# Half-height transposes in the attention, and a weight part fetched in 512-byte pieces, in a fused attention and expert kernel

## The chip, the cores and the metric

The kernel runs on one core of a Trainium2 chip. The time is device microseconds of one execution; three plain runs of the kernel before took 727.77 to 731.6 us, the median is 728.2 us. One further execution was recorded by the hardware profiler. Its engines are named PE (TensorE; PEld is its weight load, which runs beside it), DVE (VectorE), ACT (ScalarE), POOL (GpSimd) and SP (SyncE, which only issues transfers here).

## The reference, cut to what matters

```python
def _attn_ref(q, k, v):                       # 4 batches, 8 heads, 576 positions, 64 dims
    scores = scale * np.matmul(q, k.transpose(0, 1, 3, 2))
    rel = pos[:, None] - pos[None, :]
    mask_local = (rel >= 0) & (rel < 32)                              # heads 0 to 3
    mask_strided = (rel >= 0) & (pos[None, :] % 32 == pos[:, None] % 32)   # heads 4 to 7
    ...
    return np.matmul(softmax(np.where(masks, scores, -1e9)), v)

def _moe_ref(x, ...):                         # 2304 tokens, 8 experts, 512 -> 1024 -> 512
    logits = x @ w_gate + modality_bias[modality_id]
    e_idx = np.argmax(logits, axis=1)
    for e in range(E):
        h = np.maximum(x[e_idx == e] @ w1[e], 0.0)
        out[e_idx == e] = gate_w * (h @ w2[e])

def _moe2_ref(x, w_in, w_out):                # dense: 512 -> 2048 -> 512, ELU between
    h = x @ w_in
    return np.where(h > 0, h, np.exp(np.minimum(h, 0)) - 1) @ w_out
```

## The kernel before

The program has three stages. The attention takes some 110 us; the experts' stage and the dense one, which are long rows of fp32r products on TensorE, take the rest.

**Attention.** The work goes by pairs of heads: 4 batches with 4 pairs each, 16 in all, in the order `PAIRS = [2, 0, 3, 1]`, so that a strided pair (heads 4 to 7) and a local pair (heads 0 to 3) take turns. Even numbers n are strided, odd ones local. The order on every engine is the order in which the code is written, and it is pipelined by hand. Iteration n holds: `emit_S(n)`, the scores of pair n, with mask and maximum on VectorE (L1274, L1277) and the subtraction of the maximum on GpSimd (L1278); `emit_T(n + 1, 0)` and `(n + 1, 1)`, which transpose q of the next pair; `emit_PT(n - 1)`, which transposes the probabilities P of the pair before; `emit_T(n + 1, 2)` and `(n + 1, 3)` for k; `emit_PV(n - 1)`, P times v, divided by the row sums on VectorE (L1336, L1365); `emit_X(n - 2)`, which transposes the attention's result x for the router; and the exponential of pair n on ScalarE (L1283). After every fourth pair (in the local iterations 5, 9 and 13) the router's logits follow (L1413, L1424). For local pairs ScalarE first relays q and k into another layout (L1119).

A strided pair packs two heads and two halves of the rows into quarter tiles of 64 rows by 64 columns on TensorE (L1252, L1332); a full transpose takes 128 rows (L1291, L1307, L1393, L1399) or 96 (L1228, L1236). Every transpose writes to a PSUM bank, from which ScalarE or VectorE copies. The banks are handed out in turn from three tags; P's, PV's and x's share four under the tag "P":

```python
t = psum.tile([128, 512], F32, tag=tag, bufs={"S": 2, "T": 2, "P": 4}[tag], name=name)
```

**P and x before.** P of a strided pair (`sm_s`, 128 rows, 12 blocks) is transposed in six full transposes into two banks, three and then three; P of a local pair (`sm_l`, 9 blocks of 96) in nine into three banks, four, four and the tail (L1307). x of a strided pair takes six full transposes (L1393), x of a local pair four (L1399) and, for its tail, two plain 64 x 64 products with the identity (L1402) into a bank of their own; ScalarE copies both banks (L1404).

**First expert job.** After batch 1 the routing of the first two batches runs in the background of the attention (`early`). It picks the expert of the first job, gathers its tokens from DRAM on GpSimd (L467), and fetches the weights of the first blocks of 128 hidden units on SP. `fetch` issues two transfers per block, one of w1 (rows of 512 bytes, L496) and one of w2 (rows of 2 KB, L498), into one of three buffers `wraw`; ScalarE and VectorE split a buffer in a high and a low part (L489, L490), which frees it. Three fetches are issued by iteration 15, the fourth when the first split has run.

Of the kernel before, what the change touches and what calls it, by code (L numbers as in the profile page):

```python
# [19 lines left out]
B, H, S, D = 4, 8, 576, 64  # L20
# [397 lines left out]
def ffn(tc, ctx, tc_dram, x_dram, ident, router, conv, bank, w1, w2, out, run_attention):  # L418
# [75 lines left out]
    def fetch(job, f):  # L494
        raw = wr_p.tile([128, 1024], F32, tag="wraw", name="wraw")
        nc.sync.dma_start(raw[:, 0:512].rearrange("p (k n) -> p k n", k=4),  # L496
                          w1[bass.ds(job.e, 1)].rearrange("e (k p) f -> p (e k) f", p=128)[:, :, f * 128:(f + 1) * 128])
        nc.sync.dma_start(raw[:, 512:1024], w2[bass.ds(job.e, 1)].rearrange("e f d -> (e f) d")[f * 128:(f + 1) * 128])  # L498
        return raw

    def gemm1(job, f, i, ps=None):
# [570 lines left out]
def attention(tc, bg, q, k, v, mod, mbias, wg, x_dram, ident, router, bank):  # L1072
# [212 lines left out]
    def emit_PT(n):  # L1285
        if pairs[n][1] >= 2:
            sm, pt = sm_s, pt_s
            for r in range(2):
                ps = bank("P", "ps_p")
                for z in range(Z):  # L1290
                    nc.tensor.transpose(ps[:, 128 * z:128 * z + 128], sm[:, 384 * r + 128 * z:384 * r + 128 * z + 128], ident)  # L1291
                nc.scalar.copy(pt[:, Q6 * r:Q6 * (r + 1)].rearrange("p (b q) -> p b q", q=N3),
                               ps.rearrange("p (b q) -> p b q", q=D)[:, 0:6, 0:N3])
            rs = m_p.tile([128, 12], F32, tag="rs", name="rs")
            nc.vector.reduce_sum(rs, rss[n], axis=AX.X)
            bg()
            nc.vector.tensor_scalar(rs, rs, 1e-9, None, ALU.add)
            bg()
            rec = m_p.tile([128, 2, 6], F32, tag="rec", name="rec")
            nc.vector.reciprocal(rec.rearrange("p w (z r) -> p r z w", r=2), rs.rearrange("p (r z w) -> p r z w", r=2, w=2))  # L1300
            bg()
            rss[n] = rec
            return
        for at, cnt in ((0, 4), (TAIL + 1, 4), (TAIL, 1)):
            ps = bank("P", "ps_p")[0:KW, 0:128 * cnt]
            for i in range(cnt):
                nc.tensor.transpose(ps[:, 128 * i:128 * i + 128], sm_l[:, at + i], ident)  # L1307
            (nc.scalar.copy if cnt > 1 else nc.vector.tensor_copy)(pt_l[:, at:at + cnt].rearrange("p s q -> p (s q)"), ps)

    xs, stores = {}, []  # L1310

# [2 lines left out]
    def emit_PV(n):  # L1314
# [9 lines left out]
        if strided:  # L1324
            pss = [bank("P", "ps_v", 128, 6, D) for w in range(2)]
            for z in range(Z):
                for r in range(2):
                    for x in range(2):
                        for w in range(2):
                            ro = slice(64 * w, 64 * w + N3)  # L1330
                            at = (6 * r + 2 * z + x) * N3
                            nc.tensor.matmul(pss[w][64 * x:64 * x + 64, 2 * z + r], lhsT=pt_s[ro, at:at + 64],  # L1332
                                             rhs=vs[pr - 2][ro, 3 * x + z, D * r:D * r + D], start=True, stop=True)
            rec = rss.pop(n)
# [14 lines left out]
        for r in range(2):  # L1349
            for s in range(4):  # L1350
                for x in range(2):
                    nc.tensor.matmul(pss[r][64 * x:64 * x + 64, s], lhsT=pt_l[:, parts[r][0] + s, 64 * x:64 * x + 64],
                                     rhs=vl[pr][:, 2 * s + x, r], start=True, stop=True)
        for r in range(2):
            nc.tensor.matmul(pss[0][64 * r:64 * r + 64, TAIL], lhsT=pt_l[:, TAIL, 64 * r:64 * r + 64],
                             rhs=vl[pr][:, 8, r], start=True, stop=True)
        rs = m_p.tile([128, 9], F32, tag="rs", name="rs")
        for ps, (i, j) in zip(pss, parts):
# [22 lines left out]
    def emit_X(n):  # L1381

        b, pr = pairs[n]
        h0 = 2 * (pr % 2)
        x_sb = xs[b, pr // 2]
        if n + 2 >= NP:
            store_x(len(stores))
        if pr >= 2:
            for a in range(2):
                ps = bank("P", "ps_x")[:, 0:384]  # L1390
                o = ps.rearrange("p (q x z) -> p z x q", x=2, z=Z)
                for z in range(Z):
                    nc.tensor.transpose(o[:, z], x_sb[:, 2 * z + a, h0:h0 + 2].rearrange("p h d -> p (h d)"), ident)  # L1393
                nc.scalar.copy(xt[:, pr].rearrange("p j (i u a) -> p a j i u", i=R3, a=2)[:, a],
                               ps[:, 0:6 * N3].rearrange("p (i j u) -> p j i u", i=R3, u=6))
            return
        ps, pe = bank("P", "ps_x"), bank("P", "ps_xe", 128, D)
        for s in range(4):
            nc.tensor.transpose(ps[:, 128 * s:128 * s + 128], x_sb[:, 4 * s + h0:4 * s + h0 + 2].rearrange("p h d -> p (h d)"), ident)  # L1399
        for r in range(2):  # L1400
            ro = slice(64 * r, 64 * r + 64)
            nc.tensor.matmul(pe[ro], lhsT=x_sb[ro, 16 + pr], rhs=ident[ro, ro], start=True, stop=True)  # L1402
        for t, i, j in ((ps, 0, 16), (pe, 16, J)):
            nc.scalar.copy(xt[:, pr, i:j, 0:32], t.rearrange("p (j c) -> p j c", c=32))  # L1404

    lgt = const.tile([128, 2 * S], F32, name="lgt")

# [93 lines left out]
```

## Time and profile before

| what | value |
|---|---|
| median of three plain runs | 728.2 us (727.77 to 731.6) |
| profiled execution: its own time | 735.35 us |
| its span, first to last instruction | 733.6 us |
| TensorE busy | 713.0 us (97%) |
| TensorE's weight load busy | 626.4 us (85%) |
| VectorE busy | 554.4 us (76%) |
| ScalarE busy | 418.2 us (57%) |
| GpSimd busy | 120.4 us (16%) |
| TensorE's granted clock, mean | 0.984 |

The span leaves out what lies before the first and after the last instruction, 1.75 us. Ends of matmuls are modelled, so a stream of them overlaps itself: what one costs in a row is read from start to start. A clock of 1.00 is 2.4 GHz, 0.50 is 1.2 GHz; a figure between is a mean over a stretch.

### The profile page before, as it was taken

How to read it: one execution, taken by the hardware profiler on the slowest of the kernel's cores; microseconds unless marked ns; L12 is line 12 of the kernel's file. 1: busy time of each engine (PE TensorE's matmuls, PEld its weight loads, DVE VectorE, ACT ScalarE, POOL GpSimd, SP SyncE). 2: the span in 40 equal slices, each digit the busy share in tenths (PEclk: the TensorE clock that was granted, in tenths of full speed). 3: DMA queues.
4: the chain of work that ended last, by engine and by line, in shares of the span. 5: the costliest groups of instructions: out<-in, count | busy, mean ns of one | idle time of the engine just before them, and what ended most of it. 6: DMA issues, size and time to landing. Idle time of an engine off the chain costs nothing.

```text
span 733.6 us, 13503 instructions
## 1 busy us (share of the span) xinstructions
PE 713.0 (97%) x5007; PEld 626.4 (85%) x5010; DVE 554.4 (76%) x1066; ACT 418.2 (57%) x761; POOL 120.4 (16%) x182
## 2 busy tenths in 40 slices
PE   8999698999999999998999999999999999999997
PEld 5878586888888889888999899999988889989895
DVE  4777656967879877777877866787887898777773
ACT  5777465235544546455655546585556677565543
POOL 4645533122020200000000000022100003200003
PEclk9999969999999999999999999999999999999999
DMA  9999934276586676574766464166443346543302
GB/s 177 203 242 221 255 115 108 74 229 221 175 272 209 215 261 216 188 234 155 280 219 215 150 212 166 61 181 193 136 151 115 115 127 206 184 144 115 115 1 86
DMA packets 99190, 127.34 MB, mean 174 GB/s; under 512 B 20167, under 2 KB 71911, under 8 KB 99120
## 3 DMA queue, kind: packets, MB, share of 16 engines
q1 hardware_dynamic: 89136, 94.91, 43.8%
q0 software_dynamic: 9984, 31.51, 13.6%
q8 instruction: 41, 0.67, 0.4%
q14 instruction: 29, 0.24, 0.1%
HBM read 100.18 MB, written 26.21 MB: 172 GB/s over the span
## 4 chain that ended last, share of the span: by engine, by line
PE 51%; POOL 1%; issue 0%; POOLq 0%; ACT 0%
PE h_ps L719 25%; PE o_ps L810 9%; PE o_ps L809 9%; PE o_ps L808 9%; POOL out_dram L819 1%; POOLq L1497 0%; ACT y_sb L817 0%; POOLq L819 0%
## 5 line engine op out<-in xcount | busy, mean ns | idle before, releaser
L810 PE MATMUL o_ps<-wh,gl 128*128 128x512 f32 x282 | 111.2, 394 | 0.0
L809 PE MATMUL o_ps<-wl,gh 128*128 128x512 f32 x282 | 111.0, 394 | 0.0
L808 PE MATMUL o_ps<-wh,gh 128*128 128x512 f32 x282 | 110.6, 392 | 0.0
L794 ACT CAST gh<-t 128x384 fp32r<-128x384 f32 x94 | 48.3, 514 | 98.8 <-DVE t L746 95.6
L490 DVE TENSOR_TENSOR wl<-wraw,wh 128x1024 fp32r<-128x1024 f32 x56 | 68.6, 1224 | 31.4 <-ACT wh L489 29.5
L719 PE MATMUL h_ps<-xa,wh 128*128 128x384 f32 x320 | 88.1, 340 | 1.8 <-PEq L756 1.8
L745 DVE SCALAR_TENSOR_TENSOR t<-e,t 128x384 f32<-128x384 f32 x96 | 53.4, 557 | 29.2 <-ACT e L740 26.6
L870 POOL DMA_DIRECT2D wl<-wl_dram x32 | 17.5, 550 | 337.9 <-PE o_ps L810 199.6
L719 PEld LDWEIGHTS h_ps<-xa,wh 128*128 128x128 f32 x320 | 59.8, 190 | 8.3 <-issue 2.1
L800 DVE TENSOR_TENSOR gl<-t,gh 128x384 fp32r<-128x384 f32 x94 | 52.3, 556 | 18.7 <-ACT gh L794 16.9
L719 PE MATMUL h_ps<-xa,wl 128*128 128x384 f32 x192 | 65.1, 339 | 0.0
L810 PEld LDWEIGHTS o_ps<-wh,gl 128*128 128x128 f32 x282 | 52.9, 188 | 12.0
L524 PE MATMUL y_ps<-hh,wh 128*128 128x460 f32 (+1 forms) x160 | 61.4, 384 | 0.0
L526 PE MATMUL y_ps<-hh,wl 128*128 128x460 f32 (+1 forms) x160 | 60.1, 375 | 0.0
L525 PE MATMUL y_ps<-hl,wh 128*128 128x460 f32 (+1 forms) x160 | 60.0, 375 | 0.0
L489 ACT CAST wh<-wraw 128x1024 fp32r<-128x1024 f32 x56 | 58.4, 1043 | 0.0
L809 PEld LDWEIGHTS o_ps<-wl,gh 128*128 128x128 f32 x282 | 53.0, 188 | 6.3
L808 PEld LDWEIGHTS o_ps<-wh,gh 128*128 128x128 f32 x282 | 53.0, 188 | 6.2
L147 ACT ACTIVATE conv<-conv 128x512 f32<-128x512 f32 x32 | 21.8, 682 | 59.4 <-DVE conv L159 59.4
L719 PE MATMUL h_ps<-xb,wh 128*128 128x384 f32 x192 | 55.1, 341 | 0.0
L874 ACT CAST wh<-wraw 128x1024 fp32r<-128x1024 f32 x48 | 50.1, 1044 | 0.0
L719 PE MATMUL h_ps<-xc,wh 128*128 128x384 f32 x192 | 49.3, 338 | 0.0
(271 smaller groups left out, 1607.9 us busy)
## 6 DMA issues: line engine op xcount, KB each, us to landing
wraw<-w_f SPq DMA_DIRECT2D x48, 512.0 KB
wraw<-in_moe_w_dram SPq DMA_DIRECT2D x80, 256.0 KB
wl<-wl_dram POOLq DMA_DIRECT2D x32, 512.0 KB
conv<-in_moe_w_in_dram SPq DMA_DIRECT2D x16, 512.0 KB
conv<-in_moe_w_out_dram SPq DMA_DIRECT2D x16, 512.0 KB
w_f<-conv SPq DMA_DIRECT2D x32, 256.0 KB
wl_dram<-wl SPq DMA_DIRECT2D x16, 512.0 KB
qn<-in_q_dram SPq DMA_DIRECT2D x16, 288.0 KB
```

What stands on the lines that cost most here:

```text
L489: nc.scalar.copy(WH[i], raw)
L490: nc.vector.tensor_tensor(WL[i], raw, WH[i].bitcast(F32), ALU.subtract)
L524: nc.tensor.matmul(ps, lhsT=a, rhs=hh, start=f == 0, stop=False)
L525: nc.tensor.matmul(ps, lhsT=a, rhs=hl, start=False, stop=False)
L526: nc.tensor.matmul(ps, lhsT=b, rhs=hh, start=False, stop=f == NCH - 1)
L719: mm = lambda x, v, f, l: nc.tensor.matmul(ps, lhsT=x, rhs=v, start=f, stop=l, skip_group_check=on)
L745: nc.vector.scalar_tensor_tensor(t, e, 1.0, t, ALU.add, ALU.mult)
L800: nc.vector.tensor_tensor(gl, t, gh.bitcast(F32), ALU.subtract)
L808: nc.tensor.matmul(ps, lhsT=a, rhs=hi, start=first, stop=False)
L809: nc.tensor.matmul(ps, lhsT=a, rhs=lo, start=False, stop=False)
L810: nc.tensor.matmul(ps, lhsT=b, rhs=hi, start=False, stop=last)
L874: nc.scalar.copy(WH[slots(n)[nm]], wts[n, nm])
```

## The change

It has three parts, two in the attention and one in the first job's weights.

- `emit_PT` and `emit_X` transpose 64 rows at a time. For each block there are two transposes, one of the rows 0 to 63 and one of the rows 64 to 127, each with the 64 x 64 corner of the identity, and the two go to two banks in turn. P of a strided pair is 12 halves, P of a local pair 16 and one full tail, x of a strided pair 12, x of a local pair 8. Copies on ScalarE take one bank each, so one half of the rows each; the layout of `pt_s` and `pt_l` follows that, and `emit_PV` reads accordingly.
- x of a local pair uses the two banks for its tail too: each tail product goes behind the halves of one bank. ScalarE copies 256 columns of each bank, VectorE copies the tails, 64 x 64 each.
- In `fetch`, the w2 part of the first job's blocks 0 to 3 is loaded in four transfers of 128 columns (rows of 512 bytes).

```diff
@@ -495,7 +495,10 @@
         raw = wr_p.tile([128, 1024], F32, tag="wraw", name="wraw")
         nc.sync.dma_start(raw[:, 0:512].rearrange("p (k n) -> p k n", k=4),
                           w1[bass.ds(job.e, 1)].rearrange("e (k p) f -> p (e k) f", p=128)[:, :, f * 128:(f + 1) * 128])
-        nc.sync.dma_start(raw[:, 512:1024], w2[bass.ds(job.e, 1)].rearrange("e f d -> (e f) d")[f * 128:(f + 1) * 128])
+        rows = w2[bass.ds(job.e, 1)].rearrange("e f d -> (e f) d")[f * 128:(f + 1) * 128]
+        step = 128 if job.start is FIRST and f < 4 else 512
+        for i in range(0, 512, step):
+            nc.sync.dma_start(raw[:, 512 + i:512 + i + step], rows[:, i:i + step])
         return raw
 
     def gemm1(job, f, i, ps=None):
@@ -1285,12 +1288,14 @@
     def emit_PT(n):
         if pairs[n][1] >= 2:
             sm, pt = sm_s, pt_s
-            for r in range(2):
-                ps = bank("P", "ps_p")
-                for z in range(Z):
-                    nc.tensor.transpose(ps[:, 128 * z:128 * z + 128], sm[:, 384 * r + 128 * z:384 * r + 128 * z + 128], ident)
-                nc.scalar.copy(pt[:, Q6 * r:Q6 * (r + 1)].rearrange("p (b q) -> p b q", q=N3),
-                               ps.rearrange("p (b q) -> p b q", q=D)[:, 0:6, 0:N3])
+            pss = [bank("P", "ps_p") for x in range(2)]
+            for i in range(6):
+                for x in range(2):
+                    ro = slice(64 * x, 64 * x + 64)
+                    nc.tensor.transpose(pss[x][:, 64 * i:64 * i + 64], sm[ro, 128 * i:128 * i + 128], ident[ro, ro])
+            for x in range(2):
+                nc.scalar.copy(pt[:, Q6 * x:Q6 * (x + 1)].rearrange("p (b q) -> p b q", q=N3),
+                               pss[x].rearrange("p (b q) -> p b q", q=D)[:, 0:6, 0:N3])
             rs = m_p.tile([128, 12], F32, tag="rs", name="rs")
             nc.vector.reduce_sum(rs, rss[n], axis=AX.X)
             bg()
@@ -1301,11 +1306,16 @@
             bg()
             rss[n] = rec
             return
-        for at, cnt in ((0, 4), (TAIL + 1, 4), (TAIL, 1)):
-            ps = bank("P", "ps_p")[0:KW, 0:128 * cnt]
-            for i in range(cnt):
-                nc.tensor.transpose(ps[:, 128 * i:128 * i + 128], sm_l[:, at + i], ident)
-            (nc.scalar.copy if cnt > 1 else nc.vector.tensor_copy)(pt_l[:, at:at + cnt].rearrange("p s q -> p (s q)"), ps)
+        pss = [bank("P", "ps_p", KW, 8, 64) for x in range(2)]
+        for i in range(8):
+            for x in range(2):
+                ro = slice(64 * x, 64 * x + 64)
+                nc.tensor.transpose(pss[x][:, i], sm_l[ro, i + i // TAIL], ident[ro, ro])
+        pe = bank("P", "ps_pe", KW, 128)
+        nc.tensor.transpose(pe, sm_l[:, TAIL], ident)
+        for x in range(2):
+            nc.scalar.copy(pt_l[:, 0:8, 64 * x:64 * x + 64], pss[x])
+        nc.vector.tensor_copy(pt_l[:, 8], pe)
 
     xs, stores = {}, []
 
@@ -1328,7 +1338,7 @@
                     for x in range(2):
                         for w in range(2):
                             ro = slice(64 * w, 64 * w + N3)
-                            at = (6 * r + 2 * z + x) * N3
+                            at = (6 * x + 3 * r + z) * N3
                             nc.tensor.matmul(pss[w][64 * x:64 * x + 64, 2 * z + r], lhsT=pt_s[ro, at:at + 64],
                                              rhs=vs[pr - 2][ro, 3 * x + z, D * r:D * r + D], start=True, stop=True)
             rec = rss.pop(n)
@@ -1349,10 +1359,10 @@
         for r in range(2):
             for s in range(4):
                 for x in range(2):
-                    nc.tensor.matmul(pss[r][64 * x:64 * x + 64, s], lhsT=pt_l[:, parts[r][0] + s, 64 * x:64 * x + 64],
+                    nc.tensor.matmul(pss[r][64 * x:64 * x + 64, s], lhsT=pt_l[:, 4 * r + s, 64 * x:64 * x + 64],
                                      rhs=vl[pr][:, 2 * s + x, r], start=True, stop=True)
         for r in range(2):
-            nc.tensor.matmul(pss[0][64 * r:64 * r + 64, TAIL], lhsT=pt_l[:, TAIL, 64 * r:64 * r + 64],
+            nc.tensor.matmul(pss[0][64 * r:64 * r + 64, TAIL], lhsT=pt_l[:, 8, 64 * r:64 * r + 64],
                              rhs=vl[pr][:, 8, r], start=True, stop=True)
         rs = m_p.tile([128, 9], F32, tag="rs", name="rs")
         for ps, (i, j) in zip(pss, parts):
@@ -1386,22 +1396,27 @@
         if n + 2 >= NP:
             store_x(len(stores))
         if pr >= 2:
-            for a in range(2):
-                ps = bank("P", "ps_x")[:, 0:384]
-                o = ps.rearrange("p (q x z) -> p z x q", x=2, z=Z)
-                for z in range(Z):
-                    nc.tensor.transpose(o[:, z], x_sb[:, 2 * z + a, h0:h0 + 2].rearrange("p h d -> p (h d)"), ident)
-                nc.scalar.copy(xt[:, pr].rearrange("p j (i u a) -> p a j i u", i=R3, a=2)[:, a],
-                               ps[:, 0:6 * N3].rearrange("p (i j u) -> p j i u", i=R3, u=6))
+            pss = [bank("P", "ps_x", 128, 64, 6) for x in range(2)]
+            for s in range(6):
+                for x in range(2):
+                    ro = slice(64 * x, 64 * x + 64)
+                    nc.tensor.transpose(pss[x][:, :, s], x_sb[ro, s, h0:h0 + 2].rearrange("p h d -> p (h d)"), ident[ro, ro])
+            for x in range(2):
+                nc.scalar.copy(xt[:, pr].rearrange("p j (i x s) -> p x i j s", i=R3, x=2)[:, x],
+                               pss[x][:, 0:N3].rearrange("p (i j) s -> p i j s", j=J))
             return
-        ps, pe = bank("P", "ps_x"), bank("P", "ps_xe", 128, D)
+        pss = [bank("P", "ps_x", 128, 320) for x in range(2)]
         for s in range(4):
-            nc.tensor.transpose(ps[:, 128 * s:128 * s + 128], x_sb[:, 4 * s + h0:4 * s + h0 + 2].rearrange("p h d -> p (h d)"), ident)
+            for x in range(2):
+                ro = slice(64 * x, 64 * x + 64)
+                nc.tensor.transpose(pss[x][:, 64 * s:64 * s + 64], x_sb[ro, 4 * s + h0:4 * s + h0 + 2].rearrange("p h d -> p (h d)"), ident[ro, ro])
         for r in range(2):
             ro = slice(64 * r, 64 * r + 64)
-            nc.tensor.matmul(pe[ro], lhsT=x_sb[ro, 16 + pr], rhs=ident[ro, ro], start=True, stop=True)
-        for t, i, j in ((ps, 0, 16), (pe, 16, J)):
-            nc.scalar.copy(xt[:, pr, i:j, 0:32], t.rearrange("p (j c) -> p j c", c=32))
+            nc.tensor.matmul(pss[r][ro, 256:320], lhsT=x_sb[ro, 16 + pr], rhs=ident[ro, ro], start=True, stop=True)
+        for x in range(2):
+            nc.scalar.copy(xt[:, pr, 0:16, 0:32].rearrange("p (s x i) c -> p x s i c", x=2, i=2)[:, x], pss[x][:, 0:256].rearrange("p (s i c) -> p s i c", s=4, i=2))
+            ro = slice(64 * x, 64 * x + 64)
+            nc.vector.tensor_copy(xt[ro, pr, 16:J, 0:32], pss[x][ro, 256:320].rearrange("p (j c) -> p j c", c=32))
 
     lgt = const.tile([128, 2 * S], F32, name="lgt")
```

On TensorE, in iteration 8, from q's transposes of the next pair to x's of the pair two before (`qr`, `kr`: the relayed q and k; `ps_p`, `ps_pe`: banks of P; `ps_v`: of PV; `ps_x`: of x). The kernel before:

```order
L1236 MATMUL ps_tr<-ident,qr 128x96 x6
L1307 MATMUL ps_p<-ident,sm_l 96x128 x9
L1236 MATMUL ps_tr<-ident,kr 128x96 x6
L1352 MATMUL ps_v_1042<-vl_134,pt_l 64x65 x8
L1352 MATMUL ps_v_1043<-vl_134,pt_l 64x65 x8
L1355 MATMUL ps_v_1042<-vl_134,pt_l 64x65 x2
L1393 MATMUL ps_x<-ident,xs 128x2x64 x6
```

The changed kernel:

```order
L1239 MATMUL ps_tr<-ident,qr 128x96 x6
L1313 MATMUL ps_p<-ident,sm_l 96x64 x16
L1315 MATMUL ps_pe<-ident,sm_l 96x128
L1239 MATMUL ps_tr<-ident,kr 128x96 x6
L1362 MATMUL ps_v_1108<-vl_134,pt_l 64x65 x8
L1362 MATMUL ps_v_1109<-vl_134,pt_l 64x65 x8
L1365 MATMUL ps_v_1108<-vl_134,pt_l 64x65 x2
L1403 MATMUL ps_x<-ident,xs 128x64 x12
```

Nothing is moved past anything; the nine transposes of P became 16 halves and the full tail, the six of x 12 halves, and the halves of P stand between full transposes of q and k.

On VectorE, at the end of iteration 7 and the start of iteration 8 (`xs` is the attention's result, `rec` the reciprocal row sums, `xt` the transposed x, `mask_s` the strided mask). The kernel before:

```order
L1295 TENSOR_REDUCE rs<-sm_s 128x12
L1297 TENSOR_SCALAR rs<-rs 128x12
L1300 RECIPROCAL rec<-rs 128x2x3x2
L1336 TENSOR_TENSOR xs<-ps_v,rec 128x6x64 x2
L1274 TENSOR_TENSOR sm_s<-ps_sc_1206,mask_s 128x6x54
L1274 TENSOR_TENSOR sm_s<-ps_sc_1207,mask_s 128x6x54
L1277 TENSOR_REDUCE mx<-sm_s 128x12
```

The changed kernel:

```order
L1300 TENSOR_REDUCE rs<-sm_s 128x12
L1302 TENSOR_SCALAR rs<-rs 128x12
L1305 RECIPROCAL rec<-rs 128x2x3x2
L1346 TENSOR_TENSOR xs<-ps_v,rec 128x6x64 x2
L1419 COPY xt<-ps_x 64x2x32 x2
L1277 TENSOR_TENSOR sm_s<-ps_sc_1290,mask_s 128x6x54
L1277 TENSOR_TENSOR sm_s<-ps_sc_1291,mask_s 128x6x54
L1280 TENSOR_REDUCE mx<-sm_s 128x12
```

Two copies of the tails of x stand behind the multiplies of PV and ahead of the next score mask.

## Rows read from the trace of the kernel before

**Rows 1.** The page: the span, and TensorE busy in 40 slices (tenths).

```profile
span 733.6 us, 13503 instructions
...
PE   8999698999999999998999999999999999999997
```

**Rows 2.** Stretches: length; PE, PEld, DVE, ACT, POOL busy; clock; DMA share, GB/s.

```profile
40.00:60.00 20.00, 19.06 (x411) 16.48 (x404) 14.48 (x36) 16.07 (x36) 9.83 (x13) 1.00 1.06 236
...
90.00:100.00 10.00, 8.07 (x92) 5.94 (x96) 5.47 (x9) 4.97 (x12) 3.90 (x5) 0.63 0.51 154
100.00:110.00 10.00, 9.78 (x157) 8.82 (x157) 6.19 (x15) 7.40 (x15) 3.25 (x4) 0.69 0.38 114
...
120.00:130.00 10.00, 10.00 (x97) 7.32 (x96) 5.21 (x13) 5.37 (x10) 3.18 (x5) 1.00 0.55 153
```

**Rows 3.** Waits, 18 to 80 us: total us, times, longest us.

```profile
PE ps_tr L1236 <- ACT qr L1119: 1.1, 2, 0.6
...
ACT xt L1394 <- PE ps_x L1393: 4.9, 5, 1.3
...
DVE rs L1359 <- PE ps_v L1355: 5.9, 5, 1.4
```

**Rows 4.** TensorE in order of time, 64 to 70 us: start, us, operation.

```profile
64.25 1.32 PE L1424 MATMUL ps_g<-pick,lgt 128*128 128x8 f32 x10
65.50 0.92 PE L1252 MATMUL ps_sc<-kt,qt 64*64 64x54 f32 x48
...
67.06 1.19 PE L1307 MATMUL ps_p<-ident,sm_l 128*96 128x128 f32 x9
68.09 0.66 PE L1236 MATMUL ps_tr<-ident,kr 96*128 96x96 f32 x6
68.68 1.15 PE L1352 MATMUL ps_v<-vl,pt_l 96*64 96x65 f32 x32
```

**Rows 5.** TensorE's groups, 18 to 80 us: busy us, mean ns of one.

```profile
L1252 PE MATMUL ps_sc<-kt,qt 64*64 64x54 f32 x276 | 6.1, 222 | 0.3 <-issue 0.3
...
L1236 PE MATMUL ps_tr<-ident,kr 96*128 96x96 f32 x36 | 4.2, 252 | 0.0
...
L1424 PE MATMUL ps_g<-pick,lgt 128*128 128x8 f32 x18 | 2.3, 258 | 0.1
```

**Rows 6.** TensorE in order of time, iterations 7 and 8.

```profile
47.02 1.06 PE L1267 MATMUL ps_sl<-kt,qt 64*64 64x96 f32 x38
...
53.85 0.42 PE L1307 MATMUL ps_p<-ident,sm_l 128*96 128x128 f32 x2
```

**Rows 7.** VectorE in order of time, the same iterations.

```profile
48.17 1.12 DVE L1274 TENSOR_TENSOR sm_l<-ps_sl,mask_l 128x480 f32<-128x480 f32 x2 [0.41 <-PE ps_sl L1267]
...
52.88 1.02 DVE L1336 TENSOR_TENSOR xs<-ps_v,rec 128x384 f32<-128x384 f32 x2
```

**Rows 8.** VectorE's groups, 18 to 80 us.

```profile
L1308 DVE COPY pt_l<-ps_p 96x128 f32<-96x128 f32 x5 | 1.4, 277 | 0.0
...
L1368 DVE TENSOR_TENSOR xs<-ps_v,rs 128x64 f32<-128x64 f32 x5 | 1.1, 216 | 0.0
```

**Rows 9.** ScalarE's groups, 18 to 80 us.

```profile
L1404 ACT COPY xt<-ps_x 128x512 f32<-128x512 f32 x5 | 2.9, 585 | 4.3 <-PE ps_x L1399 4.3
...
L1404 ACT COPY xt<-ps_xe 128x64 f32<-128x64 f32 x5 | 1.1, 218 | 0.0
```

**Rows 10.** SP's issues in order of time, 80 to 106 us.

```profile
83.49 0.35 SPq L498 DMA_DIRECT2D wraw<-in_moe_w_dram  x1
83.95 1.19 SPq L1135 DMA_DIRECT2D vl<-in_v_dram  x2
...
87.19 1.22 SPq L498 DMA_DIRECT2D wraw<-in_moe_w_dram  x1
103.12 0.38 SPq L496 DMA_DIRECT2D wraw<-in_moe_w_dram  x1
```

**Rows 11.** TensorE in order of time, near 92 us.

```profile
91.92 0.47 PE L1228 MATMUL ps_tr<-ident,kn 96*128 96x96 f32 x3 [4.25 <-ACT qt L1232]
```

## The prediction

> **What bounds the kernel now.** The span comes first [rows 1]: the profiled execution took 735.35 us, its span 733.6 us, and the median of the three runs shown is 728.2 us, so this profile is 7.2 us longer than a plain run. The page's row of TensorE has its one low slice (6) at the fifth fortieth, 73 to 92 us, near the end of the attention. The next view is the one by stretches [rows 2]. From 40 to 60 us TensorE is busy 19.06 of 20 us, ScalarE 16.07, VectorE 14.48, at full clock; in 120 to 130 us, in the expert stage, TensorE has no gap at all (10.00 of 10), and the page's row stays at 9, once 8, from there to the last slice. So a microsecond that the attention ends earlier is kept to the end, if TensorE is what the attention waits for. The waits say for the steady part, 18 to 80 us, that it mostly is [rows 3]: ScalarE waits 4.9 us for the strided x transposes (L1393), VectorE 5.9 us for PV (L1355), while the one sizable wait of TensorE is 1.1 us for ScalarE's relay of q (L1119). The step that sets the pace is TensorE's issue, with VectorE and ScalarE close behind.
>
> **The change: transposes.** The price of a full transpose is read from start to next start [rows 4]: nine of L1307 from 67.06 to 68.09, 114 ns each. The change replaces 192 of them: 6 in each of 8 strided P, 8 in each of 8 local P (the ninth, the tail, stays), 6 and 4 in each strided and local x. Each becomes two transposes of 64 rows with 64 moving columns instead of 128, into two banks. No row of before shows a 64-row transpose, so a pair of halves is bounded:
> - below by half of 114, 57 ns, when both halves run side by side and only moving columns count;
> - the nearest rows for work side by side are the strided scores L1252, quarter tiles of 64 rows by 64 columns, four at a time: 48 in 0.92 us, one of them 222 ns [rows 4, 5], so (920 - 222) / 11 = 63 ns per group of four;
> - a weight load of 128 columns is in every half as it was in every full one. The transposes L1236 have such loads and follow each other every (660 - 252) / 5 = 82 ns, so the load takes no more than that;
> - above, if loads of the two halves follow each other, 2 x 82 = 164 ns. If a load here costs what it costs in the plain fp32 product L1424 (8 moving columns, 128-column weights, so nothing but load): (1320 - 258) / 9 = 118 ns.
>
> I take 64 ns, since L1252 shows loads of two row groups and two column groups at once, which is the harder case. That saves 50 ns on each of 192: 9.6 us.
>
> Against it stands a pause at each change of tile shape. L1236 follows L1307 0.16 us before L1307's modelled end (67.06 + 1.19); L1352, of another tile shape, starts only 0.07 us before L1236's end (68.09 + 0.66) [rows 4]: 0.09 us for a change of shape. P's halves now stand between full transposes, two changes more for each of 16 pairs: 32 x 0.09 = 2.9 us. The x halves stand where the shape changed before and after anyway. Net on TensorE: 9.6 - 2.9 = 6.7 us, or for two pairs (one strided, one local) 0.12 for strided P, 0.22 for local P, 0.30 for strided x, 0.20 for local x: 0.84 us.
>
> A rule of the Trainium skill speaks against this (TensorE: Matmul & The Clock Gate, section "LDWEIGHTS (loading the stationary operand)"): a load's time goes by its columns, not by its rows, at about columns / 1.2 ns. By it a 128-column load takes 107 ns with 64 rows too, an estimate from that page, so a pair of halves would gain 7 ns and the sum would be 1.3 - 2.9, a loss of 1.6 us. The 82 ns of L1236 [rows 4, 5] disagree with it for transposes.
>
> **How much of the 6.7 us reaches the end.** In the cycles with router work (iterations 5/6, 9/10, 13/14) TensorE has the router's products besides (L1424 alone 1.32 us [rows 4]) and the other engines have time to catch up: all of 0.84. In a cycle without it VectorE has a chain of its own. After S(7) (L1267 ends at 47.02 + 1.06 [rows 6]) VectorE works without a gap from 48.17 to 53.90 [rows 7]: mask, maximum, row sums, both multiplies of L1336, whose banks PT(7) needs. PT(7) starts at 53.85 [rows 6]. What is saved between S(7) and PT(7) (0.20 + 0.12) turns into a wait there; what is saved behind it (0.22 + 0.30 = 0.52) stays. In the new code both of PT's banks are needed at its first pair, where the second one was needed four transposes later; by [rows 7] that bank comes free at 53.90, so this costs at most 0.05 us where VectorE is as late as here. Three cycles at 0.84, four at 0.52, and 0.84 for the last strided and local pair at the seam to the expert stage: 5.4 us. In the profile the cycle 13/14 runs at half clock (0.63 and 0.69 granted on average [rows 2]), where the same transposes cost twice as much: 0.8 us more.
>
> **The change: copies.** Local x leaves 2 copies of 585 and 218 ns on ScalarE [rows 9] for two of 256 columns, which lie between these two; taking the midpoint, 0.4 us each, nothing is gained or lost. VectorE gets two copies of 64 x 64 per local pair: between 216 ns (L1368, 128 x 64) and 277 ns (L1308, 96 x 128) [rows 8], 0.43 us by the nearer one, 3.4 us in all. They stand behind L1336 and ahead of the next score mask; VectorE's next wait for TensorE is at L1359 (up to 1.4 us [rows 3]), which hides them, unless PV in its turn waits for the tail copy L1308 that stands between. In router cycles VectorE is early and that costs nothing; in the four others, where it is late, without cover, 4 x 0.43 = 1.7 us. I charge half, 0.9 us. Sum: 5.4 + 0.8 - 0.9 = 5.3 us.
>
> **The change: weight pieces.** Four fetches get three more transfers each on SP. One costs SP between 0.46 us (83.49 to 83.95) and 1.22 us (87.19) [rows 10]; at 0.6, nearer the quick one, 1.8 us a fetch and 5.4 us for the three that are issued before 88.4. Behind them on SP stand the v of the last pair and then nothing until 103.12, when the first split has freed a buffer [rows 10]: the cover is 14.7 us wide, over the 11 us that nine of the slow ones would take. The bytes are the same. I take nothing; without the cover it would be 5.4 us.
>
> **Forecast.** 728.2 - 5.3 = 722.9 us, since the terms come from stages that a plain run has as well; against the profile's own 735.35 it is 730.0.
>
> **The rivals.**
> - *VectorE and ScalarE take the gain.* For it: ScalarE 16.07 and VectorE 14.48 of 20 us [rows 2], and TensorE's wait for the relay L1119. Against it: the long waits are theirs for TensorE [rows 3]. If only what lies behind PT in half of the cycles stays, 4 x 0.52 = 2.1 us: 726 us.
> - *Load-bound halves.* If a pair of halves takes 118 ns as in L1424, it loses 192 x 4 ns and the 2.9 us: 3.7 us, 732. The skill's rule above is the same mechanism, with 107 ns: 730. Against it L1236's 82 ns.
> - *The halves do not run side by side,* so that the change does not do what it says: 164 ns a pair, 192 x 50 ns + 2.9 = 12.5 us on TensorE, at three quarters 9 us: 737 us. This decides from 114 - 2.9 / 0.192 = 99 ns a pair on. Against it L1252's 63 ns for four tiles.
> - *The weight pieces lift the stall.* At 87.7 to 91.9 us TensorE stands for 4.25 us behind a ScalarE copy [rows 11], while SP issues 2 KB rows; then the clock is halved for 7.4 + 6.2 = 13.6 us (the missing share of [rows 2]), worth 6.8 us. If smaller packets end that, up to 11 us more is gained. Against it: no row names the transfers as the cause, and a plain run, 7.2 us shorter, may not have the stall. Half of it: 717 us.
>
> **How the numbers follow.** The forecast gets 0.55 (721 to 726), the lost gain 0.20, load-bound 0.08, one after another 0.06, the lifted stall 0.10, and 0.01 remains. About 0.5% (3.6 us) is what a measurement of this kernel tells from no change; faster means below 724.6. The forecast case puts 0.44 there, the stall 0.10, the lost gain 0.03: 0.57. Slower, above 731.8, are the serial halves, half of the load-bound case and a little of the rest: 0.12. Range 716 to 731 us: it leaves out the serial halves, half of load-bound and the better part of a lifted stall. The forecast's own range, with a pair between 57 and 82 ns (8.0 to 3.2 us on TensorE), is 721 to 726.
>
> **What would show it.** Right: the 16 halves of a local P and its tail take about 8 x 0.064 + 0.11 = 0.63 us and two pauses of 0.09, where nine full ones took 1.03; the pairs of iterations in 40 to 80 us are shorter by half a microsecond or more; TensorE's wait for ScalarE's relay is no longer than now. Wrong: halves with starts 80 ns or more apart per pair; new waits of TensorE for VectorE at PT and PV of the local pairs; or a changed stretch from 85 to 110 us that outweighs all of this.

## The result: slower by 1.3%

Ten runs of the changed kernel have a median of 737.51 us (734.64 to 744.4), ten of before 728.71 us (726.22 to 734.96); the ratio of the two on record is 1.0127 with a 95% interval of 1.0091 to 1.0163 (1.0121 by the medians, 8.8 us). I had forecast 722.9 us with a range of 716 to 731. The profiled execution took 738.98 us.

Its span is 737.2 us (before 733.6 [rows 1]). Three of the stretches of [rows 2] in the changed kernel, and one more ahead of them:

```profile
20.00:40.00 20.00, 18.84 (x411) 16.05 (x406) 13.93 (x36) 13.71 (x31) 9.84 (x23) 0.84 1.01 198
40.00:60.00 20.00, 19.85 (x411) 15.92 (x409) 13.27 (x28) 12.34 (x30) 8.47 (x10) 0.79 0.87 212
90.00:100.00 10.00, 8.40 (x192) 6.99 (x192) 8.60 (x30) 5.67 (x16) 6.18 (x8) 1.00 0.67 177
100.00:110.00 10.00, 8.25 (x149) 5.71 (x147) 4.89 (x13) 7.67 (x15) 5.71 (x7) 1.00 0.84 233
```

In before's profile the half clock lay at 90 to 110 us [rows 2]. In this one it lies in the steady part instead: 0.84 at 20 to 40 and 0.79 at 40 to 60, where before had 1.00 in both, and 1.00 at 90 to 110. A stretch at 0.79 holds 8.4 us at 1.2 GHz in 20 (half of the clock is missing in 42% of it). So iterations are compared only where both kernels stand at full clock. Two such iterations lie side by side. The first is a strided one without router work (its PT, PV are those of a local pair, its x of a strided one), TensorE in order of time, before:

```profile
42.03 0.92 PE L1252 MATMUL ps_sc<-kt,qt 64*64 64x54 f32 x48
...
43.44 1.15 PE L1307 MATMUL ps_p<-ident,sm_l 128*96 128x128 f32 x9
44.42 0.66 PE L1236 MATMUL ps_tr<-ident,kr 96*128 96x96 f32 x6
45.01 1.15 PE L1352 MATMUL ps_v<-vl,pt_l 96*64 96x65 f32 x32
...
46.21 0.87 PE L1393 MATMUL ps_x<-ident,xs 128*128 128x128 f32 x6
47.02 0.31 PE L1267 MATMUL ps_sl<-kt,qt 64*64 64x96 f32 x4
...
49.99 0.93 PE L1332 MATMUL ps_v<-vs,pt_s 54*64 54x64 f32 x48
50.85 0.66 PE L1399 MATMUL ps_x<-ident,xs 128*128 128x128 f32 x4
...
51.46 0.27 PE L1252 MATMUL ps_sc<-kt,qt 64*64 64x54 f32 x2
...
53.02 0.71 PE L1236 MATMUL ps_tr<-ident,qr 96*128 96x96 f32 x6 [0.56 <-ACT qr L1119]
...
57.83 1.06 PE L1267 MATMUL ps_sl<-kt,qt 64*64 64x96 f32 x38
```

and in the changed kernel (L1313 are P's halves, L1403 and L1412 the halves of x). In both views the next iteration, a local one, and the start of the strided one behind it follow:

```profile
49.78 0.92 PE L1255 MATMUL ps_sc<-kt,qt 64*64 64x54 f32 x48
...
51.28 0.65 PE L1313 MATMUL ps_p<-ident,sm_l 64*96 64x64 f32 x16
...
52.01 0.66 PE L1239 MATMUL ps_tr<-ident,kr 96*128 96x96 f32 x6
52.65 0.33 PE L1362 MATMUL ps_v<-vl,pt_l 96*64 96x65 f32 x2
53.14 1.09 PE L1362 MATMUL ps_v<-vl,pt_l 96*64 96x65 f32 x29 [0.15 <-ACT pt_l L1317]
...
54.33 0.59 PE L1403 MATMUL ps_x<-ident,xs 64*128 64x64 f32 x12
54.85 1.06 PE L1270 MATMUL ps_sl<-kt,qt 64*64 64x96 f32 x38
...
57.78 1.17 PE L1342 MATMUL ps_v<-vs,pt_s 54*64 54x64 f32 x48
58.89 0.47 PE L1412 MATMUL ps_x<-ident,xs 64*128 64x64 f32 x8
...
59.30 0.26 PE L1255 MATMUL ps_sc<-kt,qt 64*64 64x54 f32 x2
...
61.07 0.71 PE L1239 MATMUL ps_tr<-ident,qr 96*128 96x96 f32 x6 [0.76 <-ACT qr L1122]
```

Read as distances from the first line: the iteration takes 5.07 us, before 4.99. P's transposes are shorter (0.73 from the first half to the k transposes, 0.98 before) and PV starts 0.11 us earlier, at 2.87. But its third instruction (a product is two of them here) stands until 3.36, and x starts at 4.55, before at 4.18: 0.37 us lost. X then takes 0.52 instead of 0.81: 0.29 gained. In the local iteration, whose P is that of a strided pair, x starts 4.04 us in, 3.83 before (47.02 to L1399 at 50.85), and takes 0.41 instead of 0.61 to the next scores; the whole 4.45, before 4.44. Here PV takes 1.11 us from its start to that of x, before 0.86, and the trace names no wait in it.

The 0.20 us that x gains in the local iteration is lost right behind it. The q transposes of the next strided iteration wait for ScalarE's relay of q, 0.76 us instead of 0.56, and start 2.18 us behind the start of x (58.89 to 61.07), before 2.17 (50.85 to 53.02). This iteration takes 6.61 us (59.30 to 65.91, shown below), before 6.37 (51.46 to 57.83).

TensorE's waits, 18 to 80 us, and the place of the longest, first on TensorE (L1428 is the router product), then on VectorE:

```profile
PE ps_tr L1239 <- ACT qr L1122: 1.5, 2, 0.8
PE ps_l L1428 <- DVE xt L1419: 1.2, 1, 1.2
PE ps_v L1362 <- ACT pt_l L1317: 0.3, 2, 0.2
```

```profile
65.91 1.06 PE L1270 MATMUL ps_sl<-kt,qt 64*64 64x96 f32 x38
...
70.34 0.33 PE L1415 MATMUL ps_x<-ident,xs 64*64 64x64 f32 x4
70.60 1.49 PE L1428 MATMUL ps_l<-xt,wgp 128*32 128x288 f32 x10
73.27 0.69 PE L1428 MATMUL ps_l<-xt,wgp 128*32 128x288 f32 x6 [1.18 <-DVE xt L1419]
...
75.23 0.45 PE L1255 MATMUL ps_sc<-kt,qt 64*64 64x54 f32 x16
```

```profile
70.34 1.07 DVE L1302 TENSOR_SCALAR rs<-rs 128x12 f32<-128x12 f32 x1
...
71.81 1.02 DVE L1346 TENSOR_TENSOR xs<-ps_v,rec 128x384 f32<-128x384 f32 x2
72.75 0.47 DVE L1419 COPY xt<-ps_x 64x64 f32<-64x64 f32 x2
```

The two tail copies of x have their input at 70.67 (70.34 + 0.33), but VectorE works off the row sums' reciprocals and multiplies first and comes to them at 72.75. This router iteration takes 9.32 us; in before, 57.83 (the start of the scores) to 65.50 [rows 4], 7.67.

So the round of four iterations takes 25.45 us (49.78 to 75.23), before 23.47 (42.03 to 65.50), at a granted clock of 1.00 throughout in both. Of the 1.98 us more, 0.09 lie in the first two iterations, 0.24 in the third and 1.65 in the router's. The other rounds need not lose as much: in the same profile the first router product, at half clock, does not wait, and the third waits 0.4 us.

### The profile page after: what moved, and what is told of

Same layout as the page of the kernel before. It is cut to its first block, busy times and chain, and to the rows that moved or that the text cites. A ratio compares the mean times of both kernels' runs of the same rounds, so it can differ in the third digit from the quotient of the medians.

```text
span 737.2 us, 13953 instructions
## 1 busy us (share of the span) xinstructions
PE 712.8 (97%) x5202; PEld 621.7 (84%) x5202; DVE 557.2 (76%) x1082; ACT 416.7 (57%) x761; POOL 120.3 (16%) x182
## 4 chain that ended last, share of the span: by engine, by line
PE 51%; POOL 1%; issue 0%; POOLq 0%; ACT 0%
PE h_ps L722 25%; PE o_ps L813 9%; PE o_ps L812 9%; PE o_ps L811 9%; POOL out_dram L822 1%; POOLq L1512 0%; ACT y_sb L820 0%; POOLq L822 0%
```

## The experiments

Ratios are to before on the same chip, with 95% intervals. The next two columns are means over the runs that the ratio is taken from: the granted clock, and span times the missing share of it, an upper figure for what half clock costs. The last has that figure for the runs of before on the same chip (not listed for the first row).

| run | ratio | clock | us | us, before |
|---|---|---|---|---|
| changed kernel | 1.0127 [1.0091, 1.0163] | 0.980 | 14.8 | - |
| before, unchanged | 0.9976 [0.9944, 1.0007] | 0.990 | 7.1 | 7.3 |
| pieces alone | 0.9958 [0.9928, 0.9987] | 0.991 | 6.8 | 7.3 |
| P halves | 1.0082 [1.0052, 1.0112] | 0.983 | 12.7 | 7.3 |
| x halves | 1.0088 [1.0053, 1.0123] | 0.984 | 12.0 | 7.3 |
| x halves, tails on ScalarE | 0.9998 [0.9969, 1.0027] | 0.995 | 4.0 | 5.1 |
| the same and pieces | 1.0033 [1.0003, 1.0063] | 0.989 | 8.1 | 7.3 |
| P halves, a copy on VectorE | 1.0303 [1.0266, 1.0341] | 0.978 | 16.3 | 5.1 |
| local P halves | 1.0052 [1.0020, 1.0084] | 0.987 | 9.5 | 7.3 |
| strided P halves | 1.0001 [0.9977, 1.0024] | 0.991 | 6.5 | 7.3 |
| local P halves, PV by halves | 1.0159 [1.0120, 1.0197] | 0.981 | 14.1 | 7.3 |
| before, k relay on GpSimd | 1.0017 [0.9986, 1.0048] | 0.993 | 5.2 | 5.0 |
| local P halves, k relay on GpSimd | 1.0073 [1.0038, 1.0107] | 0.988 | 9.0 | 5.0 |
| changed, tails on ScalarE | 1.0045 [1.0013, 1.0076] | 0.985 | 11.1 | 5.0 |
| changed, tails on ScalarE, k relay on GpSimd | 1.0066 [1.0033, 1.0100] | 0.982 | 13.0 | 5.0 |
| changed, zeros | 1.0131 [1.0084, 1.0177] | 0.989 | 8.5 | 5.1 |
| before, zeros | 1.0015 [0.9982, 1.0047] | 0.994 | 4.1 | 5.1 |
| changed, tails on ScalarE, zeros | 1.0022 [0.9993, 1.0051] | 0.990 | 7.6 | 8.6 |
| the same, more zeros | 1.0037 [1.0006, 1.0068] | 0.990 | 7.6 | 8.6 |

### The parts one by one

Before unchanged, and with one part of the diff each (the hunks are those of the change).

> The kernel before, unchanged, for the granted clock that goes with each of its times. Theory A (the half clock carries the loss: in the profile of the changed kernel TensorE stands at half clock for 3.4 + 13.7 + 3.4 + 3.4 us up to 124 us, 24 us of span worth about 12 us): the runs of before show a mean granted clock of 0.985 to 0.995, those of the changed kernel 0.964 to 0.991, and 0.01 of clock goes with about 7 us. Theory B (waits carry it, the clock is by the way): the clocks of both kernels overlap and the times at the same clock still differ by 5 us or more.

> Before with the weight pieces alone. Theory C (the pieces hold up SP, and the q of the second strided pair comes late: TensorE waited 2.6 us for it at 13.3 us in the changed kernel, 0.2 before): 3 to 6 us slower than before. Theories A and B (transposes and their copies): within 1.5 us of before. My prediction charged nothing for the pieces.

> Before with P in halves alone, strided and local. Theory P (both banks of P are full only at the last pair of halves, so both ScalarE copies start late and PV, which needs both from its third product on, waits: 0.35 us ahead of the local PV, 0.18 us inside the strided one): nothing gained, 0 to 4 us slower. Theory X (the loss is in the x halves): 1 to 3 us faster than before, as my prediction has it (3 of the 6.7 us lie in P).

> Before with x in halves alone, strided and local, the two tail copies on VectorE among it. Theory X (the router product waits for VectorE's copy of the tail: 1.2 us at 72 us in the changed kernel): 3 waits of 1 us or more at the router product and 2 to 5 us slower. Theory P (the loss is in P): 2 to 4 us faster.

The clocks of the two kernels' runs overlap (0.981 to 0.996 for before on this chip, 0.964 to 0.991 for the changed one on another) but the means differ: 14.8 us against 7.1 for half clock, 7.7 more and about the size of the loss. So theory A was alive. Theory C fell here: the pieces cost nothing by themselves. Theories P and X have the direction right, each half loses, but some 6 us, more than either had it (0 to 4, 2 to 5).

### Where the halves lose

X halves with their tail copies on ScalarE, P halves with one copy on VectorE:

```diff
-            nc.vector.tensor_copy(xt[ro, pr, 16:J, 0:32], ...
+            nc.scalar.copy(xt[ro, pr, 16:J, 0:32], ...
...
-                nc.scalar.copy(pt[:, Q6 * x:...
+                (nc.scalar.copy if x else nc.vector.tensor_copy)(pt[:, Q6 * x:...
```

> Before with x in halves, but the two tail copies of a local x on ScalarE instead of VectorE. Theory X (router product waits for VectorE's tail copies, 3.1 us in two waits in the x halves' profile): these waits go, and 2 to 4 us of the 0.88% are given back (1.003 to 1.006 of before). Theory A alone (the loss of the x halves is the clock, 0.984 against 0.990): within 1.5 us of the x halves with VectorE's copies, clock still 0.982 to 0.986.

> Before with P in halves, but the first of the two copies of each P on VectorE, so that both copies run at once. Theory P (PV waits for the second of two copies in a row on ScalarE): the waits of TensorE for the copies of P go (0.5 us in three waits at the local PV, 0.12 us inside each strided PV) and 1 to 3 us are given back of the 0.82%. Theory A alone: within 1 us of the P halves with ScalarE's copies, clock still 0.980 to 0.986. If VectorE is late at PT, a new wait for it of 0.3 us or more stands there and the time rises.

The first settles x: 1.0088 becomes 0.9998. That gives back more than theory X's 2 to 4 us, and the half clock goes together with the wait (12.0 us against before's 7.3, then 4.0 against 5.1). TensorE's waits for a copy of x, 18 to 80 us, are now ScalarE's and short:

```profile
PE ps_tr L1236 <- ACT qr L1119: 2.4, 2, 1.2
...
PE ps_l L1418 <- ACT xt L1407: 0.4, 2, 0.2
```

The second went its third way, further than expected: 1.0303, with waits of TensorE for VectorE's copies at both PV (18 to 80 us):

```profile
PE ps_v L1339 <- DVE pt_s L1294: 2.5, 2, 1.2
PE ps_v L1359 <- DVE pt_l L1314: 2.2, 2, 1.7
```

### The two P apart, and PV in another order

The last one goes through PV with the half outside:

```diff
-        for r in range(2):
-            for s in range(4):
-                for x in range(2):
+        for x in range(2):
+            for r in range(2):
+                for s in range(4):
```

> Before with the P of local pairs in halves alone. Theory S (ScalarE is the chain between the exponential and PV of a local pair: exponential, relay of k, two q copies, two P copies follow without a gap; with halves the third product of PV already needs the second P copy, where before the first half of PV needed the first copy only): 0.3 us lost in each of 8 iterations, 2 to 5 us with what the clock adds, 1.003 to 1.007 of before, and the wait inside PV stays. Theory A (the fewer columns of the halves let the clock fall, whichever P it is): half of the P halves' loss, 1.004, without the wait being of weight, and the other half in the strided P.

> Before with the P of strided pairs in halves alone. Theory S: 0.16 us gained at the transposes and 0.18 us lost inside PV, so no change, 0.998 to 1.002 of before. Theory A: 1.003 to 1.005.

> As the P of local pairs in halves, but PV goes through the two halves one after the other (all products of the first half's columns, then those of the second), so that its first eight products need the first copy alone. Theory S: PV starts on the first copy, the wait of 0.15 us and more behind its second product goes, and 1 to 4 us are given back: 0.998 to 1.003 of before; if products of one half are no longer side by side (62 ns each now), up to 0.5 us is lost in each of 8 iterations instead and it stays at 1.005 or above. Theory A: no change against the P of local pairs in halves.

The loss is in the local P; the strided P is even. ScalarE's copies of P in the strided iteration without router work, before and with local P halves:

```profile
44.20 1.06 ACT L1308 COPY pt_l<-ps_p 96x512 f32<-96x512 f32 x2
```

```profile
44.70 1.07 ACT L1312 COPY pt_l<-ps_p 96x512 f32<-96x512 f32 x2
```

The iteration starts at 42.03 in the one and 42.47 in the other, so the pair of copies runs from 2.17 to 3.23 us in before and from 2.23 to 3.30 with halves: shorter transposes, no earlier copies. Both end alike; what differs is when PV needs the second. Before, its first half (L1352 from 2.98) lived on the first copy. With halves the third instruction needs the second copy:

```profile
45.34 0.33 PE L1357 MATMUL ps_v<-vl,pt_l 96*64 96x65 f32 x2
45.82 1.09 PE L1357 MATMUL ps_v<-vl,pt_l 96*64 96x65 f32 x29 [0.15 <-ACT pt_l L1312]
...
47.82 0.31 PE L1267 MATMUL ps_sl<-kt,qt 64*64 64x96 f32 x4
```

It starts at 45.82, right behind the copy's end (44.70 + 1.07 = 45.77). The next scores start at 47.82, so the iteration takes 5.35 us where before's takes 4.99; eight times 0.36 is 2.9 us, of the 3.8 that 1.0052 means. In the other order PV starts at the same place and does not stand:

```profile
45.34 1.73 PE L1357 MATMUL ps_v<-vl,pt_l 96*64 96x65 f32 x29
```

The wait is gone, but from PV's start to that of x (47.28) it now takes 1.94 us, where before's PV took 1.20 (45.01 to 46.21): products of one half alone are not side by side, and the whole is slower (1.0159). That was theory S's second branch. So no run takes this wait away and gives its time back: that the loss lies in the local P is shown by the runs, that it is this wait by the trace alone.

### What stands ahead of the copies

```diff
-                nc.scalar.copy(t.rearrange("p a (h d) -> p h a d", h=2), ...
+                (nc.scalar.copy if nm == "qr" else nc.gpsimd.tensor_copy)(t.rearrange(...
```

> Before with the relay of k (0.82 us on ScalarE between the exponential and the q copies of a local pair) on GpSimd. Theory S (ScalarE's chain from the exponential to the k copies, 3.87 us in before and in the P halves alike, is what the local PV waits for or nearly): 1 to 4 us faster than before, or the same where TensorE's own work fills that stretch. If the relay comes late on GpSimd, a new wait at the k transposes and 1.005 or above.

> The P of local pairs in halves with the relay of k on GpSimd. Theory S: P's copies start 0.8 us earlier, the wait for them inside PV goes, and it is at least as fast as before with the same relay (difference 0 to -3 us), where the P of local pairs in halves alone was 4.7 us slower than before. If the loss of the local P lies elsewhere (the pauses at changes of tile shape, the clock): still 3 to 5 us slower than before with that relay.

Here theory S was wrong: with this relay too, local P halves lose 4 us (1.0073 against 1.0017). The relay is gone from ScalarE, yet the copies stand where they stood, 2.24 us behind the start of the iteration (43.25), and PV's wait with them. ScalarE in that iteration, with the P halves of TensorE, and the same two groups one strided iteration earlier:

```profile
31.82 0.65 PE L1308 MATMUL ps_p<-ident,sm_l 64*96 64x64 f32 x16
32.56 1.07 ACT L1312 COPY pt_l<-ps_p 96x512 f32<-96x512 f32 x2 [0.18 <-PE ps_p L1308]
...
44.66 0.74 ACT L1238 COPY qt<-ps_tr 128x288 f32<-128x288 f32 x2 [0.47 <-PE ps_tr L1236]
44.75 0.65 PE L1308 MATMUL ps_p<-ident,sm_l 64*96 64x64 f32 x16
45.49 1.07 ACT L1312 COPY pt_l<-ps_p 96x512 f32<-96x512 f32 x2
```

ScalarE now idles 0.47 us for the q transposes. What holds the P copies is the halves of P: both times the copies start 0.74 us behind the first half, and the earlier time the trace names the halves as what ScalarE waited for. With local P halves alone it was 0.74 us as well in the iteration shown (43.96 to 44.70). So there the chain is TensorE's q transposes, all the halves of P, which fill both banks only at their end, two P copies, PV; the relay is not in it. In the next strided iteration, behind a local one without router work, the relay did hold the copies: 1.11 us with local P halves alone (54.71 to 55.82), 0.74 with the relay moved (55.47 to 56.21). But on GpSimd it is not free: before with that relay shows a new wait of TensorE between 18 and 80 us, 2.2 us for the exponential of a strided pair.

### What is left without the tail copies

> The changed kernel with the two tail copies of a local x on ScalarE, all else as in it. If the causes found so far are the whole (VectorE's tail copies 0.9 percent, the local P 0.5, the strided P and the pieces nothing to -0.4): 1.002 to 1.007 of before, no wait of the router product for VectorE, mean clock 0.985 to 0.990. If the two parts together still lose by a less busy TensorE (theory A): 1.009 or above with a mean clock of 0.982 or less.

> The changed kernel with the tail copies on ScalarE and the relay of k on GpSimd. Theory S: the gain on TensorE that I forecast shows at last: 0.990 to 0.997 of before. Else as the changed kernel with the tail copies alone, 1.002 or above.

> Before with x in halves, the tail copies on ScalarE, and the weight pieces: the parts that cost nothing by the runs so far. If they add up (pieces alone 0.9958 with [0.9928, 0.9987], x halves with ScalarE's tail copies 0.9998 with [0.9969, 1.0027]): 0.994 to 0.999 of before. Theory C (the pieces take loads' time on SP): 1.002 or above.

Moving the tails gives back 6 us of 9 (1.0127 to 1.0045), the size of x halves' loss; the rest equals the local P's 1.0052. The relay helps here no more than above. The pieces do not add up: 0.9958 alone, but 1.0033 against 0.9998 beside the x halves, which lies in theory C's band (1.002 or above). Within some 0.4% either way their worth stays open.

X gains some 4 us on TensorE in all (eight times 0.29 and 0.20), and none of it shows in the time: 0.9998 with the tails on ScalarE. ScalarE at the seam of a local and a strided iteration, first in the changed kernel with the tails on it, then before:

```profile
53.15 0.37 ACT L1417 COPY xt<-ps_x 128x256 f32<-128x256 f32 x1 [0.99 <-PE ps_x L1415]
...
53.91 0.21 ACT L1419 COPY xt<-ps_x 64x64 f32<-64x64 f32 x1
54.14 0.83 ACT L1122 COPY qr<-qn 96x768 f32<-96x768 f32 x1
```

```profile
51.55 0.58 ACT L1404 COPY xt<-ps_x 128x512 f32<-128x512 f32 x1 [0.85 <-PE ps_x L1399]
...
52.13 0.84 ACT L1119 COPY qr<-qn 96x768 f32<-96x768 f32 x1
```

Four copies hold the relay of q for 0.99 us where two held it 0.58, and TensorE waits 1.2 us for it (up to 0.6 before [rows 3]).

### Zeros on TensorE, to raise the clock

Products of zeros into unused columns, at places where TensorE stands idle (the first two runs; the last two have theirs at the places that their texts name):

```diff
+            for _ in range((3, 0, 2, 0)[j]):
+                nc.tensor.matmul(ps[:, 288:512], lhsT=idle[:, 0:128], rhs=idle[:, 0:224], ...
```

> The changed kernel with five bf16 products of zeros (128 rows, 224 columns, into the unused columns of the same banks) in each strided iteration, three ahead of the first transposes of the next local pair, where TensorE waits for the relay of q, and two ahead of the third. They add at most 5 x 0.09 = 0.47 us of TensorE work in each of 8 iterations, 3.7 us. Theory A (half clock carries the loss: span times the missing share of the clock is 14.8 us on the mean of the changed kernel's runs, 7 us for before): the clock rises to 0.990 or more and the time falls by 4 us or more against the changed kernel, to 1.008 of before or less. Theory B (waits carry it): clock up or not, the time stays or rises by up to 3 us, 1.013 to 1.017 of before.

> Before with the same five products of zeros in each strided iteration. Theory A: before has its half clock mostly behind the stall at 82 to 95 us, which the products don't stand in the way of, so the clock stays near 0.990 and the time rises by 0 to 3 us. If it falls by 2 us or more, the fill is worth as much to either kernel and says nothing of the change.

> The changed kernel with the tail copies on ScalarE, and products of zeros where TensorE stands idle in a strided iteration: three of 224 columns ahead of the first transposes of the next local pair (it waits 1.2 us for the relay of q there) and two of 384 behind the transpose of P's tail (0.6 us from there to the next transposes). Theory A (the rest of the loss, 1.0045, is the half clock: span times the missing share is 11.1 us on the mean against 5.0 for before on the same chip, while span times clock is 2.5 us less than before's): the clock rises by 0.004 or more and the time falls to 0.996 to 1.000 of before. Theory B (the rest is waits on ScalarE, and half clock only shows that TensorE waits): 1.003 to 1.008, whatever the clock.

> The same, and the four products of zeros that a local iteration has already (2 columns each) widened to 224 columns, which adds about 0.09 us each to TensorE, 2.9 us over 8 iterations. Theory A: the clock is at least as high as with the smaller fill, and the time 0 to 3 us longer than with it, by what the products cost. Theory B: 1.005 to 1.012.

With the tails on VectorE theory A's gain does not come: the clock is 0.989, where the changed kernel alone had 0.980 on another chip, just short of the 0.990 that theory A asked for, and the time stays (1.0131). With them on ScalarE the clock, 0.990, is above that of before on the same chip (0.988, 8.6 us), and 1.0022 falls between the two theories' bands. More zeros bring no more clock and take 1.5 us more by the medians (1.0037), as theory A had it and below theory B's band. So equal clock does not bring the forecast gain, and how much of the last 0.45% is half clock and how much waits is not settled: the zeros cost something themselves (1.0015 in before, within its interval of nothing).

## Why the prediction was wrong, by its own steps

- **The price of halves was right.** For the 16 halves of a local P and its tail I had 0.63 us and two pauses of 0.09, one of them ahead of L1313; from L1313's start to the k transposes it is 0.73. The second sign that I named, iterations half a microsecond shorter, did not come, and the third, a wait for the relay no longer than now, failed (0.76 us, before 0.56). I gave every half a load of 128 columns; those of a local P have 96 (L1313, 64*96). With 128-column weights, L1403 needs 0.52 us for six pairs, pause included, 87 ns each. By the load rule of the Trainium skill that I weighed (TensorE: Matmul & The Clock Gate, section "LDWEIGHTS (loading the stationary operand)") each would be 107, an estimate from that page with the two loads of a pair side by side; this row does not agree with it.
- **X's gain was right at TensorE**: 0.29 and 0.20 us per iteration, forecast 0.30 and 0.20. In cycles without router work I had written the 0.20 off as a wait at PT for VectorE; it went into the longer wait for the relay.
- **The step that failed first: "In router cycles VectorE is early and that costs nothing."** I looked for VectorE's next wait, not for who waits for the copies. The router product needs them, and in the router cycle shown VectorE, still busy with row sums and multiplies, gets to them 2.1 us after their input. That iteration lost 1.65 us instead of 0. With the tails moved, the x halves went from 1.0088 to 0.9998, about 6.5 us with the half clock that went too.
- **The step that failed second: P's 0.22 and 0.12 us.** I costed that PT needs both banks at its first pair, and not that PV needs both copies at its third instruction. By the time x starts, 0.37 and 0.21 us are lost in the two iterations, where I had 0.22 and 0.12 gained. In the local pair's PV the trace shows the wait; in the strided pair's it shows 0.25 us more and no wait, so there the cause is not shown. For a pair of iterations without router work that makes 9.52 us against 9.43, where I had 0.52 to 0.84 less.
- **Half clock.** I gave it to the gain (0.8 us). The changed kernel has some 7 us more of it in the mean, on another chip. In x halves it went when the wait went; for the local P no run shows this. Three rounds of 1.98 us and 7.7 us of half clock, an upper figure, are more than the loss of 9 us together, so how they share it stays open.
- **ScalarE at 0** was right for the two copies of a local x, 0.54 us from the first to the relay of q (59.64 to 60.18), before 0.58. Moved there as well, the tails cost the relay 0.41 more. Of the rivals, "VectorE and ScalarE take the gain" named the place; its price, 2.1 us still kept, was wrong in sign. Weight pieces at 0 are not contradicted, and the stall they might have lifted is not in the profile of before unchanged (731.96 us), so a plain run need not have it.

## To carry to other kernels

When a producer's order changes, write down for the first instructions of each consumer which copy they need, and when that copy ends: a producer that fills two buffers side by side finishes both late. A small copy moved to another engine costs where that engine's queue stands when the reader needs it, in every kind of iteration, not in the mean. Compare iterations at equal clock, and read the clock of all runs before a wait is priced.

## Not expected of the hardware

- The products of a local PV take turns between two halves of the output partitions, and that is worth 0.74 us of 1.94.
- The clock fell where TensorE was mostly busy. Two stretches of the changed kernel, and a row of the first:

```profile
30.00:40.00 10.00, 8.97 (x176) 7.61 (x174) 6.74 (x20) 6.52 (x14) 6.33 (x13) 0.74 1.10 204
40.00:50.00 10.00, 10.00 (x131) 7.25 (x128) 5.96 (x12) 4.66 (x12) 3.90 (x5) 0.58 1.07 232
```

```profile
34.71 2.32 PE L1362 MATMUL ps_v<-vl,pt_l 96*64 96x65 f32 x31
```

In the first TensorE waited once, 0.76 us for the relay of q, which ended at 32.02; at 0.74 half of the clock is missing for 5.2 us, from about 34.8 on if it lasts to the end of the stretch, well behind that wait (the PV that starts at 34.71 takes 2.32 us, at full clock 1.09). In the second it had no gap and still stood at 1.2 GHz for most of it.
